# Hedgehog attention and Fourier mixing: the first fold on VectorE, rows first, and the mean subtraction on ScalarE

## The chip, the cores and the metric

The kernel runs on one core of one Trainium2 chip. The metric is the device time of one execution in microseconds. A core has five engines with a queue of instructions each: TensorE (PE in the profile; its weight loads are PEld), VectorE (DVE), ScalarE (ACT), GpSimd (POOL) and SyncE (SP). Here SyncE only issues transfers, and GpSimd issues transfers and computes. An engine works through its own queue in order; engines wait for one another through semaphores.

## The reference

There are 8 batches of 8 heads, 576 positions and head size 64. Attention without softmax comes first, then a Fourier mixing and a two-layer network:

```python
def phi(x):                                   # x is q or k
    proj = einsum('bhsd,df->bhsf', x, w_phi)  # 64 -> 128 features
    proj = proj - max(abs(proj), axis=-1, keepdims=True)
    return concatenate([exp(proj), exp(-proj)], axis=-1)
kv  = einsum('bhsf,bhsd->bhfd', phi(k), v)
z   = sum(phi(k), axis=2)
x   = einsum('bhsf,bhfd->bhsd', phi(q), kv) / (einsum('bhsf,bhf->bhs', phi(q), z)[..., None] + 1e-06)
# heads side by side: x is (8, 576, 512)
u   = x + real(fft(fft(x, axis=1), axis=2))
un  = (u - mean(u)) / sqrt(var(u) + 1e-06)    # over the last axis
out = u + maximum(un @ w_ch1, 0) @ w_ch2      # 512 -> 2048 -> 512
```

## The kernel before, in words

**Batches and streams.** A batch's work is cut into streams of small steps, each a Python generator. `PLAN`, a string with one letter per step, is the order in which all steps of all batches are recorded, and so the order of every engine's queue: nothing is reordered afterwards. Letters that matter here: `F` the two-layer network (`forward`, 68 steps), `M` the heads and the mixing (`mixing`, 26 steps), `D` the second fold (`fold_later`), `N` mean subtraction and transposes (`normalise`, one step per chunk of rows), `U` the scales (`scales`), `K`, `V`, `Q` the loads, `T` the exponentials of keys and queries, `R` and `P` the maxima, `S` the scaling of the values, `Y` matmuls on ones whose result nobody uses. While the network of one batch runs, the plan puts the attention and mixing of the next one between its steps.

**Rows.** A batch's 576 rows lie in five chunks of up to 128 partitions, in an order in which chunks 0 and 2, and 1 and 3, hold mirrored rows. X (128 x 5 x 513, f32) holds them all; its last column is a spare one.

**Attention.** `keys`, `queries` and `qmax` project on TensorE, ScalarE makes the exponentials KPp, KPn, QPHP, QPHN, VectorE takes maxima, GpSimd multiplies the values by the keys' scales into VCp, VCn, V4P, V4N (L460, L475). `keyvalue` sums kv (L896); a ScalarE copy makes it kvh. `combine` (L1018) multiplies a head's queries with it; VectorE adds and inverts (L1029, L1034, L1036), GpSimd writes the head's 64 columns of X (L1037).

**Mixing.** The real part of the two Fourier transforms is computed by matrix products with cosine and sine tables after folding: entries that share a cosine are added, those that share a sine subtracted, so that the products are half as large. From batch 1 on, GpSimd folds columns first (L1002): as soon as heads h and 7 - h stand in X, it writes their sums and differences to FEO (128 x 5 x 2 x 256, f32), two instructions of 320 elements each per pair of heads. VectorE then folds rows (`fold_rows`, L909 and L913) in two steps `D`. In batch 0 VectorE makes both. ScalarE copies one row to HI, TensorE spreads it over all partitions (pm, L1062), VectorE subtracts it (L1066), and a second fold along columns makes CEO (L1075). TensorE multiplies by the tables along rows (psD, L1086) and along columns (pu, L1141); VectorE adds the result to X (L1131), which now holds u.

**Normalise.** For each chunk, in the order 0, 2, 1, 3, 4, VectorE takes mean and variance (L1210, L1211) and, from batch 1 on, subtracts the mean into UN, in bf16 with columns reversed on both sides (L1186); SyncE issues a DMA that writes UN transposed to UT (L1203). Batch 0 subtracts with ScalarE (L1181, one chunk with VectorE) and transposes on TensorE. The scale 1/sqrt(var + 1e-06) is made by GpSimd with an addition (L1223) and a power (L1224), twice per batch: for chunks 0 and 2, and for all five.

**Network.** `hidden(0, 256)` multiplies UT of chunks 0 and 2 with W1b (psf, L1253) in 16 groups of four matmuls; ScalarE clips each group to HT (L1257). `output(0)`, `output(2)` follow, then `hidden(256, 576)` and the other three outputs (pso, L1264; the last chunk L1289). VectorE scales and adds to X (L1270, L1296), and SyncE stores the chunk: eight DMAs for chunk 1 (L1234), one or two for the others. psf, pso and pu share three PSUM buffers (`pb`), projections two others (`pj`).

**Loads.** GpSimd issues the loads of the next batches (L289): K in three pieces, V in six, Q in four.

Of the kernel before, what the change touches and what calls it, by code (L numbers as in the profile page):

```python
# [10 lines left out]
ALU = mybir.AluOpType  # L11
# [12 lines left out]
    "CYYYYYCZGZGTGRZZTZGGJKKTSTJRTPTRPYTQKSRJTYQPTJTRJMWTMPSSTPTPTMMTMTTPSCMMMTMVMMTMQTHYVMMMVMHHMHYYMYYZ"  # L24
    "MDDBMYAMHTMMVHRWMTMTNTMMTYYNNMNKSNFRFNFNFFUTFFFURSNTMTPFFNFUFMRTSPFTFRTNMSFFUFVTKQUMFFFMTFFSMFVKQTPT"
    "MFQUFFTBFPPMTPUAMTFFPMMFFMTFFMRFTFMFRFFFMFTFQFFMFPFMFFFFPFPFTFDFDQRKFFMVFTFMTFYFKVFTVMFFTMVKFRSSRMFT"
    "PPMTFTMNQNTFMSMSSBMMVTFTFMUTPMTMFNFMFNFMFFNFTUMFFFPTFFMKVFMMFFFMFFMFFFAMTRTVFFMRTSFFFFFFMFFFFTMVRFFF"
    "FTQPDFFFTPFFRDFFFTMKPQFFTMFKFFMMFFSRFMTFFVFMTTMTNNVFTFFFSFFMMMMTFMFBTPPQMSFFTFFTSPUNKMNFFVMFFMFFPNFF"
    "UMTFKFMFMFMFFFMFFFMFAMFFTRTFFMSFFFFQFRMFFTFFFTPRFFFFTMFFFTPDKFFFFDFFFRTMVTFFFMFMFQFFMVSRMFFFMTTTMTFF"
    "VNTMFSFNMVMMFTFFMTPSFFTBSFFVUMTPPFMFFFNNMTFPQFNFMFFUMFFKMFFPMFFKMFFMFFMFFAMFFFMTRTFFFMFFFRFFTMFFFTPF"  # L30
    "FFQRFDTFKPFFDFFFMQMFTFFMFFRMSFFTVTFMSRFFFMVTTTMTFNNMMVFMMFFSFTBMVNTTFTFSMFPFSUFFTFMTFFMNPPQPFMFKFFMF"
    "NFMUFKFPFMMFFAFFMFMFQFFTTMFFFRFSFMFFFFRFMFFFTFTPRFVFFFFMTFFDQKFPTRFFFDFFFVTMTFFFMFQMMSRFFTFFMFTTFVMT"
    "MFNFNFMMVSFTSMMTTFTFMFBTFTFFPFUMSFFMPPNPVNVAMFFFMFFMNFFMFFPMMFFFFFMFFMFTMRFFFTPSFFFFMFFFFVRMFFTFFTVP"
    "RFFFFMTDFFUFTPFFRFDFFFVTMTFFFMFMFFFMMFSRFTFMFMTNSTNTFSMMFFMMFTFFNMTTTFFFFNPPUMFFSTNMFFFMFFMTPFMFFUFP"
    "FFFMMFFFMFFMFFMFFMFMFFFMFFFFFFFMFFFFFFFDDFFFFMFFFMFMFFMMFFMFFMNNFFFFMUFFFMFFFFFFFMFFNFNFNFFFFFUFFFFF"
    "FFFFFFFFFFFFFFFFFFFFFFFFFFFFFFFFFFFFFFFFFFFFFFFFFFFFF"
# [4 lines left out]
def kernel(  # L41
# [41 lines left out]
    mhalf = const.tile([128, 5], F32, name="mhalf")  # L83
    nc.vector.memset(mhalf[:], -0.5)
# [41 lines left out]
    warm = const.tile([128, 1], F32, name="warm")  # L126
    keep = const.tile([128, 1], F32, name="keep")
# [163 lines left out]
    def make_k(b):  # L291
        KS = stage.tile([128, H, 256], BF16, tag="KS", name="KS")
        KS4 = stage.tile([64, H, D], BF16, tag="KS4", name="KS4")
        pieces = [(KS4[:], k[b, :, 512:576, :].rearrange("h p d -> p h d"))]
        for g in range(2):
            hs = slice(4 * g, 4 * g + 4)
            pieces.append(
                (KS[:, hs, :], k[b, hs, 0:512, :].rearrange("h (p j) d -> p h (j d)", j=4))
            )
        return (KS, KS4), pieces  # L300
# [606 lines left out]
    def fold_rows(FEO, lo, hi):  # L907
        odd = slice(max(lo, 1), hi)
        nc.vector.tensor_tensor(  # L909
            out=FEO[:, 2:4, 1, odd], in0=FEO[:, 0:2, 1, odd], in1=FEO[:, 2:4, 1, odd],  # L910
            op=ALU.subtract,
        )
        nc.vector.tensor_tensor(  # L913
            out=FEO[:, 2:4, 0, lo:hi], in0=FEO[:, 0:2, 0, lo:hi], in1=FEO[:, 2:4, 0, lo:hi],
            op=ALU.add,
        )
        if lo == 0:
            nc.gpsimd.tensor_tensor(
                out=FEO[:, 2:4, 1, 0], in0=FEO[:, 0:2, 1, 0], in1=FEO[:, 2:4, 1, 0], op=ALU.add
            )  # L920

    def first_heads():
        X = xpool.tile([128, 5, C + 1], F32, tag="X", name="X")
        FEO = fpool.tile([128, 5, 2, 256], F32, tag="FEO", name="FEO")
        CEO = fpool.tile([128, 3, 2, 2, 128], BF16, tag="CEO", name="CEO")
        HI = HIS[0]

        def rows_folded():
            nc.scalar.copy(out=HI[0:1, :, 1:128], in_=FEO[0:1, 0, :, 1:128])
            fold_rows(FEO, 1, 128)  # L930
            yield
# [479 lines left out]
```

## Time and profile before

| | us |
|---|---|
| median of 7 runs | 436.16 (433.82 to 439.5) |
| profiled execution | 436.59 |
| its span, first to last instruction | 434.8 |
| busy in it: TensorE | 406.7 |
| VectorE | 337.4 |
| ScalarE | 289.3 |
| GpSimd | 283.5 |
| mean granted TensorE clock | 0.979 |

Matmuls are pipelined, so a busy TensorE is not TensorE at its full pace. The idle time that a group shows is the engine's wait just before it, with what ended it. Instructions that only issue a transfer on SyncE are not counted as busy, but they take time on that queue. A clock of 0.50 in a stretch means that matmuls there ran at half speed.

### The profile page before, as it was taken

The numbers are of one execution on the slowest core, as the hardware profiler recorded it, in microseconds if no ns is written. First come the engines' busy times: TensorE is split into PE (matmuls) and PEld (weight loads), VectorE is DVE, ScalarE is ACT, GpSimd is POOL, SyncE is SP. The second block draws the span as 40 slices with busy tenths as digits, with TensorE's granted clock in tenths as the row PEclk, the third lists the DMA queues.
The fourth block names the chain that finished last, engine by engine and source line by source line (L and its number), as shares of the span: only waits on it lengthen the run. The fifth ranks groups of instructions, "written<-read, shape, count | busy, mean of one in ns | idle before, by whom it ended". The sixth has DMA issues, their size and how long they took to land.

```text
span 434.8 us, 10443 instructions
## 1 busy us (share of the span) xinstructions
PE 406.7 (94%) x4110; PEld 257.1 (59%) x4110; DVE 337.4 (78%) x643; ACT 289.3 (67%) x620; POOL 283.5 (65%) x386
## 2 busy tenths in 40 slices
PE   8699889999599999999999999999999989999993
PEld 3356466644285657665676558565766567656561
DVE  6978865799969988788979898887889796759102
ACT  2788799727664977577856897498757785344340
POOL 7886356898938976887579488797468453901100
PEclk9789999999889999999999999999999999999997
DMA  8999874939494398938692779938863171104304
GB/s 216 177 181 183 129 110 47 173 42 154 92 113 78 48 129 125 153 51 92 117 160 45 74 117 125 114 53 117 118 111 50 20 105 32 26 0 79 65 22 84
DMA packets 108962, 42.70 MB, mean 98 GB/s; under 512 B 83185, under 2 KB 103793, under 8 KB 108913
## 3 DMA queue, kind: packets, MB, share of 16 engines
q0 software_dynamic: 46272, 16.60, 35.4%
q1 hardware_dynamic: 62481, 25.38, 30.9%
q8 instruction: 32, 0.52, 0.5%
q14 instruction: 17, 0.14, 0.1%
q10 hardware_dynamic: 160, 0.07, 0.1%
HBM read 36.77 MB, written 9.44 MB: 106 GB/s over the span
## 4 chain that ended last, share of the span: by engine, by line
PE 55%; DVE 24%; ACT 9%; POOL 6%; DMA 3%; issue 1%; DVEq 0%; POOLq 0%; ACTq 0%
PE psf L1253 23%; PE pso L1264 17%; DVE X L1131 4%; DVE UN L1186 3%; DMA UT<-UN 3%; PE psD L1086 3%; POOL FEO L1002 2%; ACT HT L1257 2%; PE kv L896 2%; DVE st L1210 2%; POOL X L1037 1%; DVE CEO L1075 1%; ACT KPp L506 1%; PE psk L500 1%; DVE cb L1034 1%
## 5 line engine op out<-in xcount | busy, mean ns | idle before, releaser
L1253 PE MATMUL psf<-UT,W1b 128*128 128x320 bf16 (+1 forms) x1024 | 143.0, 288 | 8.4 <-DVE X L1296 4.2
L1257 ACT ACTIVATE HT<-psf 128x256 bf16<-128x256 f32 (+1 forms) x256 | 101.4, 417 | 53.9 <-PE psf L1253 45.9
L1264 PE MATMUL pso<-W2b,HT 128*128 128x512 bf16 x512 | 126.0, 379 | 0.0
L1253 PEld LDWEIGHTS <-W1b 128*128 128x128 bf16 x1024 | 95.2, 98 | 36.9 <-issue 8.0
L1264 PEld LDWEIGHTS <-HT 128*128 128x128 bf16 x512 | 45.7, 98 | 44.7 <-issue 2.5
L1037 POOL TENSOR_TENSOR X<-cb,rd 128x320 f32<-128x320 f32 x56 | 40.3, 726 | 22.8 <-DVE rd L1036 22.1
L475 POOL TENSOR_TENSOR VCn<-VS,VCn 128x512 bf16<-128x512 bf16 x28 | 29.7, 1060 | 30.7 <-ACT VCn L470 25.6
L1002 POOL TENSOR_TENSOR FEO<-X 128x320 f32<-128x320 f32 x56 | 46.3, 847 | 2.2
L1270 DVE SCALAR_TENSOR_TENSOR X<-pso,rs,X 128x512 f32<-128x512 f32 x32 | 23.6, 736 | 31.0 <-PE pso L1264 30.9
L506 ACT ACTIVATE KPn<-psk 128x1024 bf16<-128x1024 f32 x28 | 28.5, 1020 | 16.8 <-DVE MK L520 16.8
L564 DVE TENSOR_REDUCE MQ<-psq 128x8 f32<-128x1024 f32 (+1 forms) x32 | 34.3, 1087 | 4.9 <-PE psq L556 4.6
L506 ACT ACTIVATE KPp<-psk 128x1024 bf16<-128x1024 f32 x28 | 28.7, 1025 | 9.0 <-PE psk L500 8.9
L520 DVE TENSOR_REDUCE MK<-psk 128x8 f32<-128x1024 f32 x28 | 33.8, 1207 | 0.7 <-ACT KPp L506 0.6
L615 ACT ACTIVATE QPHP<-psh 128x1024 bf16<-128x1024 f32 x28 | 29.1, 1040 | 4.5 <-PE psh L606 4.4
L289 POOL DMA_DIRECT2D VS<-in_v_dram x42 | 30.1, 722 | 0.4 <-POOL VCp L475 0.3
L475 POOL TENSOR_TENSOR VCp<-VS,VCp 128x512 bf16<-128x512 bf16 x28 | 30.2, 1080 | 0.0
L615 ACT ACTIVATE QPHN<-psh 128x1024 bf16<-128x1024 f32 x28 | 29.4, 1048 | 0.0
L1210 DVE BATCH_NORM_STATS2 st<-X 128x6 f32<-128x512 f32 (+1 forms) x40 | 27.2, 680 | 0.0
L1223 POOL TENSOR_SCALAR VE<-MV 128x2 f32<-128x2 f32 (+1 forms) x16 | 5.7, 354 | 32.8 <-DVE MV L1211 31.9
L1186 DVE TENSOR_SCALAR UN<-X,MV 128x512 bf16<-128x512 f32 (+1 forms) x35 | 25.4, 727 | 1.3
L1131 DVE TENSOR_TENSOR X<-pu,X 128x512 f32<-128x512 f32 (+3 forms) x49 | 23.2, 527 | 3.6 <-PE pu L1141 3.4
L289 POOL DMA_DIRECT2D QS<-in_q_dram x28 | 23.8, 855 | 1.4 <-DMA QT<-QS 1.4
(460 smaller groups left out, 807.2 us busy)
## 6 DMA issues: line engine op xcount, KB each, us to landing
out_dram<-X SPq DMA_DIRECT2D x16, 256.0 KB
out_dram<-X SPq DMA_DIRECT2D x64, 64.0 KB
KS<-in_k_dram POOLq DMA_DIRECT2D x14, 256.0 KB, 5.0
QS<-in_q_dram POOLq DMA_DIRECT2D x14, 256.0 KB, 5.2
VS<-in_v_dram POOLq DMA_DIRECT2D x28, 128.0 KB, 3.8
W1b<-in_moe_w_ch_dram POOLq DMA_DIRECT2D x1, 2048.0 KB, 15.8
W2b<-in_moe_w_ch_dram POOLq DMA_DIRECT2D x1, 2048.0 KB, 15.4
W2b<-in_k_dram SPq DMA_DIRECT2D x2, 512.0 KB
```

Source lines behind the costliest of these rows:

```text
L289: nc.gpsimd.dma_start(out=pieces[i][0], in_=pieces[i][1])
L475: nc.gpsimd.tensor_tensor(out=VC[:, hs, :, 0:D], in0=values[b][0][:, hs, :].rearrange("p h (j d) -> p h j d", d=D), in1=VC[:, hs, :, D:D + ...
L506: nc.scalar.activation(out=KP[:, hs, :, :].rearrange("p e (jp jj) f -> p jj (e jp) f", jj=2), in_=psk[:], func=AT.Exp, scale=sgn,)
L615: nc.scalar.activation(out=o, in_=psh[:], func=AT.Exp, scale=sgn)
L1002: nc.gpsimd.tensor_tensor(out=FEO[:, :, i, a:a + D], in0=X[:, :, a:a + D], in1=X[:, :, C - a:C - a - D:-1], op=op,)
L1037: nc.gpsimd.tensor_tensor(out=X[:, :, D * h:D * h + D], in0=cb[:, :, 0:D], in1=rd[:].to_broadcast([128, 5, D]), op=ALU.mult,)
L1131: nc.vector.tensor_tensor(out=to, in0=more, in1=to, op=ALU.add)
L1186: nc.vector.tensor_scalar(out=UN[0:M, c, ::-1], in0=X[0:M, c, C - 1::-1], scalar1=mv[0:M, c, 0:1], scalar2=None, op0=ALU.subtract,)
L1210: nc.vector.bn_stats(out=st[0:M, :], in_=X[0:M, c, 0:C])
L1253: nc.tensor.matmul(ps[:], lhsT=W1b[:, cc, 128 * hh:128 * hh + 128], rhs=UT[:, cc, lo:hi], start=(cc == 0), stop=(cc == NCC - 1),)
L1257: nc.scalar.activation(out=HT[:, hh, lo:hi], in_=ps[:], func=AT.Relu)
L1264: nc.tensor.matmul(po[:], lhsT=HT[:, hh, at:at + 128], rhs=W2b[:, hh, :], start=(hh == 0), stop=(hh == NHH - 1),)
```

## The change

- **First fold.** From batch 1 on GpSimd's folds by pairs of heads go. For all batches `folded` runs on VectorE, rows first: four steps `D` instead of two. The first two add and subtract the mirrored chunks for the outer and the inner columns (four instructions of 512 elements), the third folds the single chunk 4 along columns and lets ScalarE copy the row to HI in two parts, the fourth folds the rest along columns. The result R is 128 x 3 x 2 x 512.
- **Subtraction.** From batch 1 on VectorE only negates the mean (nm), and ScalarE subtracts: one instruction per chunk.
- **Loads and scales.** K comes in two pieces, V in four; there is one power per batch from batch 1 on, and the addition before it is VectorE's.
- **Order.** `PLAN` is another string: 1236 steps instead of 1253, since some streams have fewer. Heads are combined in the order 0, 7, 1, 6, 4, 2, 5, 3 instead of 4, 0, 7, 1, 6, 2, 5, 3.

```diff
-    def fold_rows(FEO, lo, hi):
...
+    def folded(X, R, HI):
+        by_row = (ALU.add, ALU.subtract)
+        quarters = X[:, :, 0:C].rearrange("p c (a n) -> p c a n", n=128)
+        for cs in (slice(0, 4, 3), slice(1, 3)):
+            for i, op in enumerate(by_row):
+                nc.vector.tensor_tensor(
+                    out=R[:, 0:2, i, :].rearrange("p c (a n) -> p c a n", n=128)[:, :, cs],
+                    in0=quarters[:, 0:2, cs], in1=quarters[:, 2:4, cs], op=op,
+                )
+            yield
+        for i, op in enumerate(by_row):
+            nc.vector.tensor_tensor(
+                out=R[:, 2, i, 1:256], in0=X[:, 4, 1:256], in1=X[:, 4, 511:256:-1], op=op
+            )
+            nc.vector.tensor_tensor(
+                out=R[:, 2, 0, 256 * i:256 * i + 1], in0=X[:, 4, 0:1], in1=X[:, 4, 256:257], op=op
+            )
+        flat = HI[0:1].rearrange("p i n -> p (i n)")
+        nc.scalar.copy(out=flat[:, 0:257], in_=R[0:1, 2, 0, 0:257])
+        nc.scalar.copy(out=flat[:, 257:512], in_=R[0:1, 2, 1, 1:256])
+        yield
+        for i, op in enumerate(by_row):
+            nc.vector.tensor_tensor(
+                out=R[:, 0:2, i, 1:256], in0=R[:, 0:2, i, 1:256], in1=R[:, 0:2, i, 511:256:-1],
+                op=op,
+            )
...
-        def fold(h):
-            a = D * h
-            for i, op in enumerate((ALU.add, ALU.subtract)):
-                nc.gpsimd.tensor_tensor(
-                    out=FEO[:, :, i, a:a + D], in0=X[:, :, a:a + D],
-                    in1=X[:, :, C - a:C - a - D:-1], op=op,
-                )
...
-        nc.vector.scalar_tensor_tensor(
-            out=flat[0:65, 4, :], in0=flat[0:65, 4, :], scalar=keep[0:65], in1=pm[0:65],
-            op0=ALU.mult, op1=ALU.subtract,
-        )
+        for i, n in ((0, 257), (1, 255)):
+            nc.vector.scalar_tensor_tensor(
+                out=R[0:65, 2, i, i:i + n], in0=R[0:65, 2, i, i:i + n], scalar=keep[0:65],
+                in1=pm[0:65, 257 * i:257 * i + n], op0=ALU.mult, op1=ALU.subtract,
+            )
...
                 measure(b, c)
-                nc.vector.tensor_scalar(
-                    out=UN[0:M, c, ::-1], in0=X[0:M, c, C - 1::-1], scalar1=mv[0:M, c, 0:1],
-                    scalar2=None, op0=ALU.subtract,
+                nm = small.tile([128, 1], F32, tag="nm", name="nm")
+                nc.vector.tensor_scalar_mul(out=nm[0:M, :], in0=mv[0:M, c, 0:1], scalar1=-1.0)
+                nc.scalar.activation(
+                    out=UN[0:M, c, :], in_=X[0:M, c, 0:C], func=AT.Identity, bias=nm[0:M, :]
                 )
...
+            if b and first:
+                continue
...
-            nc.gpsimd.tensor_single_scalar(out=VE[:], in_=mv[:, cs, 1], scalar=1e-06, op=ALU.add)
+            nc.vector.tensor_single_scalar(out=VE[:], in_=mv[:, cs, 1], scalar=1e-06, op=ALU.add)
...
-        values[b], pieces = make_v(b, 4)
-        for which in ((0, 1), (2,), (3,), (4,), (5,)):
+        values[b], pieces = make_v(b, 2)
+        for which in ((0, 1), (2,), (3,)):
...
-        "F": (forward, 68), "M": (mixing, 26), "D": (fold_later, 2), "N": (normalise, 5),
-        "U": (scales, 2), "P": (part(0), 7), "T": (part(1), 18), "R": (part(2), 5),
-        "S": (part(3), 5), "K": (fetch_k, 3), "V": (fetch_v, 5), "Q": (fetch_q, 3),
+        "F": (forward, 68), "M": (mixing, 26), "D": (fold_later, 4), "N": (normalise, 5),
+        "U": (scales, 1), "P": (part(0), 7), "T": (part(1), 18), "R": (part(2), 5),
+        "S": (part(3), 5), "K": (fetch_k, 2), "V": (fetch_v, 3), "Q": (fetch_q, 3),
```

## The prediction

> **What bounds the kernel now.** I read the page's busy shares and clock row first, then TensorE's waits, then the timeline around the longest wait, then SyncE's timeline, and the groups by shape last.
>
> ```profile
> PE 406.7 (94%) x4110; PEld 257.1 (59%) x4110; DVE 337.4 (78%) x643; ACT 289.3 (67%) x620; POOL 283.5 (65%) x386
> PEclk9789999999889999999999999999999999999997
> ```
>
> TensorE is busy nearly always; VectorE is second. The clock row dips in three places: slices 2 and 3, slices 11 and 12, the end.
>
> The chain of waits ends in TensorE alone. It gives TensorE's pace when nothing holds it:
>
> ```profile
> 397.33 6.29 PE psf L1253 x56
> 403.62 6.91 PE pso L1264 x32
> 410.53 8.69 PE psf L1253 x64
> ```
>
> So 112 ns for 256 columns, 136 for 320, 216 for 512. Both kernels issue the same matmuls (the same counts of every shape in their built orders), so the time changes only by how long TensorE is held. Its waits, longest first (us in total, times, longest):
>
> ```profile
> PE psf L1253 <- DVE X L1296: 4.2, 1, 4.2
> PE psf L1253 <- DMA UT<-UN: 2.8, 5, 0.9
> ...
> PE psD L1086 <- DVE CEO L1075: 1.9, 3, 1.1
> ```
>
> The single large one is in batch 1. VectorE and TensorE there (start, duration; the bracket is the idle time before):
>
> ```profile
> 112.57 4.65 DVE L1186 TENSOR_SCALAR UN<-X,MV 128x512 bf16<-128x512 f32 x1
> 117.14 1.93 DVE L1131 TENSOR_TENSOR X<-pu,X 128x512 f32<-128x512 f32 x4
> 119.00 1.52 DVE L1296 SCALAR_TENSOR_TENSOR X<-pso,rs,X 64x512 f32<-64x512 f32 x2
> ```
> ```profile
> 119.80 1.44 PE L1253 MATMUL psf<-UT,W1b 128*128 128x256 bf16 x6 [4.24 <-DVE X L1296]
> ```
> ```profile
> 112.74:116.15 3.41, 1.98 (x40) 1.32 (x38) 3.41 (x1) 3.38 (x8) 3.41 (x5) 1.00 0.27 44
> 116.15:122.98 6.83, 3.18 (x23) 2.43 (x24) 6.69 (x11) 1.03 (x3) 4.23 (x6) 0.50 0.79 60
> ```
>
> One mean subtraction took 4.65 us while GpSimd ran six products on end. The last two lines (stretch, then busy PE, PEld, DVE, ACT, POOL, granted clock) show GpSimd busy throughout, and the clock at 0.50 from 116.15 to 122.98. The subtraction's usual price (min/median/max ns), and that of two-input folds by shape (busy us, mean ns | idle before):
>
> ```profile
> L1186 DVE TENSOR_SCALAR UN<-X,MV x35: 478/486/4649, 110.8 to 401.5; 128x512 bf16<-128x512 f32 x28, 64x512 bf16<-64x512 f32 x7
> ```
> ```profile
> L1075 DVE TENSOR_TENSOR CEO<-FEO 128x384 bf16<-128x384 f32 x24 | 13.0, 568 | 0.2
> L913 DVE TENSOR_TENSOR FEO<-FEO 128x384 f32<-128x384 f32 x7 | 6.4, 920 | 0.0
> ```
>
> From batch 2 on, the transposes of the first chunks stand on SyncE's queue behind eight stores of one chunk:
>
> ```profile
> 158.45 5.93 SPq L1234 DMA_DIRECT2D out_dram<-X  x8
> 164.49 2.59 SPq L1203 DMA_TRANSPOSE UT<-UN  x2
> ```
>
> The second UN had ended at 162.57 (162.06 + 0.51), 1.9 us before its queue was free.
>
> **The change part by part.** The sum is made against the profiled execution's own 436.59 us (span 434.8 and 1.8 around it); it stands 0.43 above the median of 436.16.
>
> *Mean subtraction to ScalarE, batch 1.* In the changed order VectorE runs, from the first addition after the second projection to the second chunk's mean: additions 0.68 + 0.15 + 0.68, statistics 0.68 + 0.18, the new negation 0.15 (nm rows of batch 0: 135 to 152 ns), a 64-row maximum 1.21, statistics 0.86, negation 0.15: 4.74. Then UN on ScalarE, 0.72 (batch 0's row, 707 to 743 ns), behind half an exponential of 1.04, then 2.58 to the first psf (119.80 less 117.22). From 108.60, where those additions start, that is 117.16 instead of 119.80: **-2.6**; -3.2 with nothing in front, -2.1 behind a whole exponential. What is late next is this same transpose, TensorE waiting about 1.6.
>
> *The clock.* 3.18 us of matmuls after 119.80 ran at 0.50: 1.6 lost. The ends are 0 (the drop came after a stretch in which TensorE was busy only 1.98 of 3.41, partly because ScalarE was full) and -1.6. I take **-1.6**: the stall that filled the slow stretch mostly goes, and the changed order puts the last block of four filler matmuls (0.86) between these projections.
>
> *Mean subtraction, batches 2 to 7.* VectorE loses 28 times 789 less 486 ns, 8.5 us in all, to blocked subtractions; 4.2 of it is the one above. The rest gives TensorE nothing: the first two chunks wait for SyncE, whose stores are in the same place in the changed queue. Behind these transposes on SyncE stand K's and the last stores, which a late UN would hold too. If the cover goes, two UNs on ScalarE behind an exponential cost at most 1.8 per batch. TensorE's work between the end of the output that those stores follow and the first psf, at the paces above, is 9.1, 8.8, 8.9, 8.6, 8.4 us for batches 2 to 6 before and 9.8, 8.3, 8.8, 9.3, 8.1 after: even. **0**; ends -2.8 (the whole transpose wait) and 6 times 1.8 = +10.8.
>
> *ScalarE's new work.* Five UNs of 0.72 per batch, seven batches: 25 us on 289. Two chunks lie in the projections; three fall mostly into the next batch's first hidden layer, where each psf group (four matmuls, 0.44) waits for a ScalarE eviction (0.39) and has three buffers. Two spare buffers cover 0.88: one UN alone, but not UN plus exponential (1.76), 0.88 short. Ends: 0, and three such meetings in each of six batches, 15.8. By the windows ScalarE idles a quarter of the time (178.8 busy of 250 from 125 to 375), so I take one meeting in twelve: **+1.3**.
>
> *Folds.* Off GpSimd go 56 folds (46.3 us), 7 corner sums (3.0) and 7 column copies (1.3). On VectorE, per batch: four of 512 elements, between the unblocked rows of 384 (0.55) and 640 (0.82), 0.68 each; two of 255 at 0.41 (batch 0's rows of 254 and 256); two of 510 at 0.68; four tiny at 0.15 (the two-column additions); the subtraction of pm in two of about 0.45 for one of 0.74. That is 5.5 plus 0.2. It loses the old row folds, 0.74 + 0.92 + 0.28 + 0.28 = 2.2, and UN, 25.4/7 = 3.6, and gains five negations and one epsilon, 0.9: +0.8 per batch on an engine idle 16% (209.6 of 250, so 7.5 us in a period of some 47). The path from the last head's product to pm was 1.69 (two GpSimd folds) + 0.56 + 0.61 (HI) = 2.9; it becomes 1.36 + 1.12 + 0.8 (two HI copies at the 0.41 of a one-row copy) = 3.3, and the new last fold step, 1.7, runs beside HI and pm and adds about 0.8 ahead of the CEO folds. TensorE's order leaves 9.9, 9.1, 9.9, 6.0, 8.0, 6.0 us there (7.2, 5.9, 7.7, 5.4, 5.3, 6.0 before), 1.9 more on average than it had. **0**; ends -1.9 (the CEO wait goes) and +4: if GpSimd blocks four folds on the path, each by 0.53 (what separates blocked and free L913, 1.08 and 0.55), 2.1 per batch against 1.9 of new cover leaves 0.2, or 0.6 where only 1.5 is new, in seven batches.
>
> Here a rule speaks against the change. The row: L913 averages 920 ns where L1075 of the same 384 elements averages 568. The Trainium skill (SBUF — State Buffer, "SBUF: two separate sides") says VectorE instructions with two SBUF inputs and GpSimd share one port pair as an exclusive lock, held for a whole instruction, and that the loser waits it out. By the rule alone every fold on the path may lose a whole product of 0.73: four make 2.9 per batch against 1.9 of new cover, +7, and 440.3. By the rows only some pairs meet a product, and it stays at 433.3.
>
> *Fewer loads, one root.* Three DMA issues (0.72 to 0.80 each) and one root (0.74) less per batch on GpSimd, and the epsilon: 3.3 us. GpSimd sets no TensorE wait in the list; **0**. SyncE's transposes of K now wait for one larger load, whose issue stands early enough; at worst the 5.0 us landing of 256 KB doubles, still before its use a batch later. The single root's scales are due only at the first output, eight steps of the forward pass later.
>
> *Start, batch 0.* The 512-element mask on VectorE took 3.04 (10.55 to 13.59) while GpSimd cleared six buffers; a 960-element one took 0.66. The changed GpSimd order issues a load after three of them: -1.3 (0 to -2.3). Against it: the last fold runs 4.0 instead of 3.06 before pm's subtraction (+0.9), and ScalarE copies HI ahead of three of the four sine tables, so that their 2.3 us and the next table load stand between HI and the next evictions (+0.4; 0 to +1.8). **0**; ends -2.3 and +2.7.
>
> Sum: -2.6 - 1.6 + 1.3 = -2.9; 433.7 beside the own 436.59, **433.3** beside the median.
>
> **Rivals.** *ScalarE becomes what holds the hidden layers* (slower). For it: only 0.05 us of spare per group. Against: ScalarE's idle quarter. At one and a half short meetings per batch (1.3 us) it costs 7.9 in six batches, less 4.2: **439.8**. It decides from 0.7 per batch on, where it eats the gain. *The stall re-forms*: ScalarE's exponentials, full in 112.74 to 116.15 (3.38 of 3.41), make the second UN as late as the lock did, the clock drops again, and SyncE hides the rest: **436.2**. *The port lock falls on the folds*: the +4 above in place of 0: **437.3**, or nearer 434 if half of them meet a product.
>
> **How the numbers follow.** A measurement tells about 0.5% from no change, 2.2 us. Forecast 0.45 (0.38 faster, 0.07 same); ScalarE 0.27 (0.25 slower); re-formed stall 0.18 (0.12 same, 0.04 slower); lock 0.10, spread evenly. Faster 0.42, same 0.25, slower 0.33. The forecast's own range, from its ends for stall and start, is 430 to 435.5; with the cases of both signs it is 428.5 to 441.
>
> **What would show it.** Right: no TensorE wait over 2.5 us in batch 1, no clock of 0.50 between batch 0's start and the end, UN at 0.72 on ScalarE, GpSimd near 205 us busy, folds of 512 near 0.68. Wrong: waits of psf for HT or for UN above 1 us in several batches; folds of 512 near 1.2; the start later than now at the first psf.

## The result and the profile after

The changed kernel takes 438.25 us (median of 14 runs, 436.66 to 439.15), the kernel before 436.23 us in 35 runs beside it: a ratio of 1.0041, with a 95% interval of 1.0024 to 1.0057. That is slower by 0.4%, inside the 2.2 us (0.5%) within which the prediction counts a time as the same. It had forecast 433.3, faster, with 430 to 435.5 as the range of the forecast. The profiled execution took 437.48 us, its span is 435.7.

The page of the changed kernel: the busy shares, the clock row, and the group of the moved mean subtraction (busy us, mean ns | idle time of ScalarE just before it, and what ended it).

```profile
PE 406.1 (93%) x4110; PEld 254.7 (58%) x4110; DVE 339.8 (78%) x720; ACT 308.4 (71%) x661; POOL 208.6 (48%) x269
PEclk9999999999999999999999999999999999999998
L1152 ACT ACTIVATE UN<-X,nm 128x512 bf16<-128x512 f32 (+1 forms) x35 | 25.0, 723 | 10.7 <-DVE nm L1151 9.9
```

Nearly everything that was to show the forecast right is there: UN costs 0.72 us on ScalarE, GpSimd is busy 208.6 us (near 205 was said), and the clock row has no dip between its ends. TensorE's waits (us in total, times, longest) no longer hold the 4.2 us of batch 1:

```profile
PE psf L1220 <- DMA UT<-UN: 3.8, 4, 1.6
PE psD L1050 <- DVE CEO L1039: 1.9, 4, 0.7
...
PE psk L496 <- DVE cb L1004: 0.9, 2, 0.5
...
PE psh L602 <- ACT KPn L502: 0.7, 1, 0.7
...
PE pm L1026 <- ACT HT L1224: 0.7, 1, 0.7
...
PE psk L496 <- ACT KPn L502: 0.4, 1, 0.4
```

No single wait stands out; there are more short ones. The timeline around batch 1's projections, where one subtraction had taken 4.65 us on VectorE and TensorE had stood 4.24 us, now reads (start, duration; the bracket is the idle time before):

```profile
109.21 0.72 ACT L1152 ACTIVATE UN<-X,nm 128x512 bf16<-128x512 f32 x1
111.14 1.08 POOL L471 TENSOR_TENSOR VCp<-VS,VCp 128x512 bf16<-128x512 bf16 x1
111.28 0.72 ACT L1152 ACTIVATE UN<-X,nm 128x512 bf16<-128x512 f32 x1 [0.44 <-DVE nm L1151]
114.76 1.47 PE L1220 MATMUL psf<-UT,W1b 128*128 128x256 bf16 x10
```

The second subtraction ran beside a GpSimd product (111.14) in its usual 0.72, and the first psf followed without a long wait. TensorE's pace at the end of the chain is the old one (64 psf in 8.69 us), and on SyncE the eight stores still stand ahead of the first transposes, here in batch 3:

```profile
411.47 8.69 PE psf L1220 x64
```
```profile
200.07 5.13 SPq L1201 DMA_DIRECT2D out_dram<-X  x8
205.30 3.62 SPq L1168 DMA_TRANSPOSE UT<-UN  x2
```

The second subtraction ended at 205.19 on ScalarE (204.47 + 0.72), just as the queue came free (200.07 + 5.13 is 205.20): in this batch the cover that the prediction counted on held, with nothing to spare. So the stall is gone, and yet the kernel is not faster. The milestones tell why. The table gives the start of each batch's first psf by the two timelines, in us:

| batch | 0 | 1 | 2 | 3 | 4 | 5 | 6 | 7 | span |
|---|---|---|---|---|---|---|---|---|---|
| before | 55.1 | 119.8 | 168.4 | 213.9 | 261.5 | 308.4 | 355.2 | 395.6 | 434.8 |
| after | 52.2 | 114.8 | 162.8 | 210.3 | 260.9 | 306.4 | 354.9 | 396.7 | 435.7 |

The changed kernel leads by 2.9 us at batch 0's first psf, by 5.0 at batch 1's and 5.6 at batch 2's, and has lost it all by batch 7. The matmuls ahead of batch 1's first psf are the same work in both orders (about 80.1 and 79.8 us at the paces of 112, 136 and 216 ns for 256, 320 and 512 columns and estimated ones for the small products), so that point cuts both kernels into comparable halves: **119.8 and 315.0 us before, 114.8 and 320.9 after; 5.0 gained, 5.9 lost.** The cut puts the 3.2 us at half clock behind the old stall (119.8 to 122.98) into the second half of the kernel before. The prediction priced them at 1.6, and the changed kernel has no such drop, so what else it lost there is nearer 7.5 than 5.9. In the second half I took each matmul's end, less the end of the one before it and its own pace, and put what was left down to the engine that had released it: what ScalarE ended rose from 3.0 to 6.8 us, what the transposes on SyncE ended from 3.8 to 4.5, and what VectorE ended by 0.9 to 1.6, depending on the pace taken for the small products.

### The profile page after: what moved, and what is told of

Read it like the earlier page. It is cut to its first block, busy times and chain, and to the rows that moved or that the text cites. A ratio compares the mean times of both kernels' runs of the same rounds, so it can differ in the third digit from the quotient of the medians.

```text
span 435.7 us, 10470 instructions
## 1 busy us (share of the span) xinstructions
PE 406.1 (93%) x4110; PEld 254.7 (58%) x4110; DVE 339.8 (78%) x720; ACT 308.4 (71%) x661; POOL 208.6 (48%) x269
## 4 chain that ended last, share of the span: by engine, by line
PE 48%; DVE 31%; ACT 13%; DMA 3%; POOL 3%; issue 2%; DVEq 0%; POOLq 0%; ACTq 0%; SPq 0%
PE psf L1220 22%; PE pso L1231 12%; DVE cb L1004 4%; DVE tg L999 3%; DMA UT<-UN 3%; DVE MK L516 2%; DVE R L908 2%; DVE X L1095 2%; PE kv L892 2%; PE psD L1050 2%; ACT HT L1224 2%; DVE X L1237 2%; DVE st L1175 2%; ACT KPn L502 2%; ACT QPHN L611 1%
## 5 line engine op out<-in xcount | busy, mean ns | idle before, releaser
L1224 ACT ACTIVATE HT<-psf 128x256 bf16<-128x256 f32 (+1 forms) x256 | 100.0, 416 | 34.2 <-PE psf L1220 26.9
L502 ACT ACTIVATE KPn<-psk 128x1024 bf16<-128x1024 f32 x28 | 28.6, 1022 | 13.8 <-DVE MK L516 13.7
L1152 ACT ACTIVATE UN<-X,nm 128x512 bf16<-128x512 f32 (+1 forms) x35 | 25.0, 723 | 10.7 <-DVE nm L1151 9.9
L456 POOL TENSOR_TENSOR V4N<-VS,V4N 64x256 bf16<-64x256 bf16 x14 | 8.9, 638 | 48.1 <-ACT V4N L452 34.5
L1191 POOL TENSOR_TENSOR rs<-VE,mhalf 128x5 f32<-128x5 f32 (+1 forms) x9 | 10.3, 1139 | 33.5 <-DVE VE L1190 33.5
L992 PEld LDWEIGHTS <-QPHP 128*128 128x128 bf16 x280 | 20.8, 99 | 5.6 <-DVE cb L1004 2.1
```

The costliest lines, as they stand in the source:

```text
L502: nc.scalar.activation(out=KP[:, hs, :, :].rearrange("p e (jp jj) f -> p jj (e jp) f", jj=2), in_=psk[:], func=AT.Exp, scale=sgn,)
L1224: nc.scalar.activation(out=HT[:, hh, lo:hi], in_=ps[:], func=AT.Relu)
```

## The experiments

The theory that came out of this: moving the subtraction to ScalarE made ScalarE's other evictions late (A, G in the texts below). Rivals: waiting at the head of ScalarE's queue (F), VectorE's new folds (C, H), and the changed order of steps itself (B, I, J, K). All kernels were timed beside the kernel before; for most, the two halves of its profiled span are given too, cut at batch 1's first psf. The halves are of one execution, the time is the median of several: the profiled one took 3.8 us more than the median in the first run below, 2.9 more with the folds alone in the old order, 1.9 more with only the folds on GpSimd, 4.8 more in "before, then changed" and 2.0 less with the subtraction back on VectorE.

### The subtraction, in both orders

*All of it on ScalarE, in the order of before.*

```diff
-                nc.vector.tensor_scalar(
-                    out=UN[0:M, c, ::-1], in0=X[0:M, c, C - 1::-1], scalar1=mv[0:M, c, 0:1],
-                    scalar2=None, op0=ALU.subtract,
-                )
+                nm = small.tile([128, 1], F32, tag="nm", name="nm")
+                nc.vector.tensor_scalar_mul(out=nm[0:M, :], in0=mv[0:M, c, 0:1], scalar1=-1.0)
+                nc.scalar.activation(
+                    out=UN[0:M, c, :], in_=X[0:M, c, 0:C], func=AT.Identity, bias=nm[0:M, :]
+                )
```

> The kernel before with one thing done: the mean subtraction of batches 1 to 7 as a negation on VectorE and an activation on ScalarE; its order of steps, folds, loads and roots kept. The prediction's terms for this part alone were -2.6 (batch 1's stall), -1.6 (clock) and +1.3 (ScalarE): 433.3. Theory A: the stall and the clock go, but ScalarE costs 3.8 and not 1.3: 435.8 (434.5 to 437). Rival B (order is what costs): the gain stands whole, 432. Both expect no TensorE wait over 2.5 us in batch 1; if the stall is still there, the lock was not its cause.

Measured: 452.97 us, ratio 1.0386 (1.0357 to 1.0416); halves 117.5 and 337.4. Neither theory had it. In the profiled execution the first half gains 2.3 us and the second loses 22, of which 3.8 is that execution's distance from the median. The timeline of this run in batch 2 shows the mechanism:

```profile
169.55 0.15 DVE L1187 TENSOR_SCALAR nm<-MV 128x1 f32<-128x1 f32 x1
...
169.74 0.72 ACT L1188 ACTIVATE UN<-X,nm 128x512 bf16<-128x512 f32 x1 [2.56 <-DVE nm L1187]
...
170.37 0.25 ACT L904 CAST kvh<-kv 128x130 bf16<-128x130 f32 x1
...
170.67 0.40 PE L896 MATMUL kv<-VCp,KPp 128*128 128x65 bf16 x4 [2.64 <-ACT kvh L904]
```

ScalarE had nothing to do for 2.56 us. The subtraction stood first in its queue and waited for the negated mean, which VectorE reached late (a maximum of 1.23 and the statistics came first); the copy of kvh, 0.25 us of work that was ready, stood behind it; and TensorE stood 2.64 us for kvh. Over the run this wait is the largest:

```profile
PE kv L896 <- ACT kvh L904: 13.7, 12, 3.8
```

The clock adds to it: it stood at 0.51 from 169.6, within the wait shown, to 176.5, and again from 323.2 to 330.1; from batch 2 on the kernel before has no such drop until its end.

*The same, over 64 of 512 columns.*

```diff
-                    out=UN[0:M, c, :], in_=X[0:M, c, 0:C], func=AT.Identity, bias=nm[0:M, :]
+                    out=UN[0:M, c, 0:64], in_=X[0:M, c, 0:64], func=AT.Identity, bias=nm[0:M, :]
```

> The kernel before with the mean subtraction on ScalarE in all seven batches, but over 64 of 512 columns only (seven eighths of the subtraction are left out): ScalarE's work for it falls from 25 us to about 9, while each one still waits for VectorE's negated mean, with what stands behind it in ScalarE's queue. The full one gave 453.0, 16.4 us over the kernel before, and ScalarE stood idle 16.5 us ahead of subtractions. Theory F (the queue's head waiting is the cost): 446 to 451. Rival G (ScalarE's added work is the cost): 437 to 441.

Measured: 447.10 us, ratio 1.0244 (1.0220 to 1.0268); halves 117.2 and 327.6. The short activation took 0.35 us, so ScalarE lost some 12 us of work (it is busy 296.1 us instead of 308.6), and 5.9 of the 16.4 us went. 10.7 us over the kernel before stayed: most of the price is waiting at the head of the queue, as theory F said, and a third is the work. The group's idle time in this run shows that the waiting did not shrink with the work, it grew (16.5 us in 18 waits before the cut):

```profile
  DVE nm L1189: 21.1, 24
```

*ScalarE's subtraction cut in the changed order.* The same edit, made in the changed kernel.

> The changed kernel with the subtraction over 64 of 512 columns only (seven eighths left out): ScalarE loses some 16 us of its 308, its queue's waits for the negated mean (9.9 us) stay. Theory G (added work on ScalarE makes its evictions late): 434.5 (433 to 436). Theory F (waiting at the queue's head), or that the order is what costs: 437 to 438.3.

Measured: 437.95 us, ratio 1.0036 (1.0020 to 1.0051); halves 115.0 and 321.0, the second that of the changed kernel to a tenth. ScalarE is busy 298.4 us instead of 308.4. Theory A/G falls: in the changed order these 10 us of ScalarE's added work cost TensorE nothing that can be measured. ScalarE's waits for the negated mean stayed (9.3 us here, 9.9 in the changed kernel), so this run does not price them.

*The subtraction back on VectorE, in the changed order* (the first diff of this section, reversed).

> The changed kernel with one thing undone: the mean subtraction of batches 1 to 7 back on VectorE, in the changed order. In the changed kernel's trace the waits of TensorE that end with a ScalarE instruction came to 6.8 us from batch 1's first psf on, against 3.0 before (+3.8); those that end with VectorE to 4.4 against 2.8 (+1.6). Theory A (the subtraction on ScalarE makes evictions late): the +3.8 goes, the time falls to 434.5 (433 to 436), with ScalarE-ended waits near 3. Rival B (the new order of steps is what costs, whichever engine subtracts): 438, no change from the changed kernel. Rival C (VectorE is what holds TensorE, so that 35 more instructions of 0.49 to 0.79 there cost more than they save on ScalarE): 440 or more, VectorE-ended waits over 6.

Measured: 449.30 us, ratio 1.0281 (1.0256 to 1.0305); halves 116.1 and 329.4. It is 11 us slower than the changed kernel, so A falls here too, but not to C as it was put: what VectorE ended has one large entry.

```profile
160.13 4.86 DVE L1150 TENSOR_SCALAR UN<-X,MV 128x512 bf16<-128x512 f32 x1
160.62 1.06 POOL L471 TENSOR_TENSOR VCn<-VS,VCn 128x512 bf16<-128x512 bf16 x1
161.63 1.05 POOL L471 TENSOR_TENSOR VCp<-VS,VCp 128x512 bf16<-128x512 bf16 x1
162.65 1.05 POOL L471 TENSOR_TENSOR VCn<-VS,VCn 128x512 bf16<-128x512 bf16 x1
163.66 1.05 POOL L471 TENSOR_TENSOR VCp<-VS,VCp 128x512 bf16<-128x512 bf16 x1
...
165.71 0.62 PE L1255 MATMUL pso<-W2b,HT 128*64 128x512 bf16 x2 [5.03 <-DVE X L1095]
```

The stall of batch 1 has come back, in batch 2: again one subtraction sits on VectorE until GpSimd's run of products ends (164.7), and TensorE stands 5.03 us. The clock stood at 0.50 for 3.4 us behind it (165.8 to 169.2). These two make most of the 8.5 us by which this run's second half is the longer one.

*Only batch 1's first two subtractions on ScalarE, in the order of before.*

```diff
+                if b == 1 and c in (0, 2):
+                    nm = small.tile([128, 1], F32, tag="nm", name="nm")
+                    nc.vector.tensor_scalar_mul(out=nm[0:M, :], in0=mv[0:M, c, 0:1], scalar1=-1.0)
+                    nc.scalar.activation(
+                        out=UN[0:M, c, :], in_=X[0:M, c, 0:C], func=AT.Identity, bias=nm[0:M, :]
+                    )
+                else:
+                    nc.vector.tensor_scalar(
...
```

> The kernel before with the mean subtraction on ScalarE for batch 1's first two chunks alone. With all 35 on ScalarE in this order the stretch from batch 0's last output to batch 1's first hidden-layer product was 1.8 us shorter (13.1 to 11.3). If the stall and the clock were worth what the prediction said: -2.6 - 1.6, so 432. If only what that stretch showed, and the clock's drop goes too: about 434. Rival: ScalarE's two subtractions put the projections' and batch 1's features behind them, and the time is 436 or more.

Measured: 434.21 us, ratio 0.9935 (0.9911 to 0.9959); halves 117.6 and 314.8. The stall itself is worth 2.2 us. The clock's drop did not go (columns: stretch, then busy PE, PEld, DVE, ACT, POOL, granted clock, DMA share, GB/s):

```profile
111.67:115.08 3.41, 1.41 (x16) 0.69 (x17) 3.07 (x6) 3.41 (x8) 3.36 (x4) 1.00 0.67 95
115.08:121.91 6.83, 6.09 (x61) 4.76 (x61) 5.01 (x10) 4.29 (x11) 5.73 (x9) 0.51 0.78 137
```

TensorE is still busy only 1.41 of 3.41 us there, now because ScalarE is full (3.41 of 3.41) and its exponentials are late, and the next 6.83 us run at 0.51. The clock dropped behind TensorE's idle time in that stretch, though something else had caused it.

### The two orders

*The changed operations in the old order, and the folds alone in it.* Both use the old PLAN with each letter D written twice. The first has the changed operations, with empty steps where they need fewer; two powers per batch are kept:

```diff
-        "U": (scales, 1), "P": (part(0), 7), "T": (part(1), 18), "R": (part(2), 5),
-        "S": (part(3), 5), "K": (fetch_k, 2), "V": (fetch_v, 3), "Q": (fetch_q, 3),
+        "U": (scales, 2), "P": (part(0), 7), "T": (part(1), 18), "R": (part(2), 5),
+        "S": (part(3), 5), "K": (fetch_k, 3), "V": (fetch_v, 5), "Q": (fetch_q, 3),
...
-    LONGER = {("N", 0): 10, ("U", 0): 7, ("M", 0): 24, ("T", 0): 20}
+    LONGER = {("N", 0): 10, ("U", 0): 7, ("M", 0): 29, ("T", 0): 20}
```

The second is the kernel before with the changed `folded` and the heads that call it:

```diff
-        "F": (forward, 68), "M": (mixing, 26), "D": (fold_later, 2), "N": (normalise, 5),
+        "F": (forward, 68), "M": (mixing, 26), "D": (fold_later, 4), "N": (normalise, 5),
```

> The changed kernel's operations in the order of steps of the kernel before (the two steps of the row folds doubled to four, empty steps where there are fewer, two roots per batch kept since one would come too late in batch 5). Theory A: the subtraction on ScalarE and the folds cost the same or more without an order made for them: 438 to 442. Rival B: the old order is the better one, so 433 or less.

> The kernel before with the folds alone moved to VectorE, in its order (the two steps of the row folds doubled to four at their place; subtraction, loads and roots as before). All of the change in this order was 28.8 us over the subtraction alone (481.8 against 453.0), with TensorE waiting 12.1 us at pm for evictions ahead of the copy of HI. Theory J (parts priced by the order they stand in): 450 to 462, the waits at pm there without any subtraction on ScalarE. Rival (the two parts only hurt together): under 442.

Measured: all of the change 481.81 us, ratio 1.1017 (1.0991 to 1.1043), halves 123.0 and 357.0; the folds alone 461.19 us, ratio 1.0569 (1.0542 to 1.0597), halves 127.3 and 335.0. The second is what theory J expected; for the first, neither theory came near. So in the order of before the folds cost 25 us, the subtraction 16, and all together 45. With the folds alone, the waits are at pm, as theory J said:

```profile
PE pm L1036 <- ACT HT L1231: 12.0, 5, 2.9
PE pm L1036 <- ACT HI L926: 4.9, 2, 2.8
```

The clock is part of the 25 us: its mean over this run is 0.957, against 0.979 before. In that order pm comes too early for a fold chain on VectorE. By the trace the time from the last head's product on GpSimd to the end of the second HI copy was 5.2 to 7.5 us in batches 1 to 6, since up to three maxima of 1.2 stand between the folds on VectorE, and TensorE stood 1.7 to 2.9 in each. In the changed kernel the same chain took 3.1, 7.3, 6.8, 7.7, 3.4, 4.4 and 3.3 us in batches 1 to 7, and TensorE stood at most 0.65 for pm. This is the cover that the prediction worked out (5.3 to 7.7 us of TensorE work ahead of pm before, 6.0 to 9.9 after), and the changed order does supply it. The chain's price of 3.3 us was too low: with it, the old order would have covered the folds as well.

*The operations of before in the changed order, and the folds alone put back in it.* The changed PLAN; the folds of before, in four steps of which two are empty, and, from the second of these kernels on, the changed order of heads:

```diff
-        order = (4, 0, 7, 1, 6, 2, 5, 3)
-        ready = {7: (0,), 6: (1,), 5: (2,), 3: (3,)}
+        order = (0, 7, 1, 6, 4, 2, 5, 3)
+        ready = {6: (1,), 4: (0,), 5: (2,), 3: (3,)}
```

> The kernel before with all its operations (folds on GpSimd, subtraction on VectorE, more loads, two roots) in the changed order of steps; steps that are now fewer are joined, and where there are more a step is empty. Rival B: the order costs some 4 us by itself, 440. Theory A: nothing of the +3.8 is there; 435 (433 to 438), the GpSimd folds falling in other places are the open part. A stall of one subtraction behind GpSimd products may turn up in another place.

> All operations of the kernel before in the changed order, with the heads taken in the changed order (in the first attempt head 4 came ahead of its features and took those of the batch before). Theory J: 450 to 460, most of it in stalls behind GpSimd; if the order alone were the loss: 440.

> The changed kernel with the folds alone put back on GpSimd (with VectorE's row folds, as before), in the changed order and its order of heads. Theory H (VectorE's fold work costs some 5 us here): 433 if GpSimd had room; but the steps are placed for folds of VectorE, so the fold of the last head now comes after two more GpSimd products in the queue ahead of pm: theory J (a part is priced by the order it stands in) says 445 to 455, with TensorE or VectorE waiting for GpSimd's FEO.

Measured: 458.71 us with the old order of heads (1.0496, 1.0474 to 1.0519), where head 4 comes ahead of its own features, and 458.22 (1.0503, 1.0489 to 1.0516) with the changed order of heads; 440.49 us with only the folds on GpSimd (1.0106, 1.0089 to 1.0123; halves 115.6 and 324.9). The first two say that neither order is the better one by itself: the old operations lose 22 us in the new order (the first of these runs had been expected at 440 at most), and the new ones 45 in the old. The third is a surprise in its smallness: it was expected at 445 to 455, and is 2.2 us over the changed kernel. VectorE is the better place for the folds in this order, but by little.

### What the lost half is made of

*The folds cut to an eighth.*

```diff
-    def folded(X, R, HI):
+    def folded(X, R, HI, n=128):
...
-                    in0=quarters[:, 0:2, cs], in1=quarters[:, 2:4, cs], op=op,
+                    in0=quarters[:, 0:2, cs, 0:n], in1=quarters[:, 2:4, cs, 0:n], op=op,
...
-                out=R[:, 0:2, i, 1:256], in0=R[:, 0:2, i, 1:256], in1=R[:, 0:2, i, 511:256:-1],
+                out=R[:, 0:2, i, 1:2 * n], in0=R[:, 0:2, i, 1:2 * n], in1=R[:, 0:2, i, 511:512 - 2 * n:-1],
...
-        folds[b] = folded(X, R, HI)
+        folds[b] = folded(X, R, HI, 16)
```

> The changed kernel with VectorE's folds of batches 1 to 7 cut: those of 512 elements to 64, those of 510 to 62 (seven eighths of them are left out), the instructions and their order the same. VectorE loses about 3 us per batch, 20 in all. With the subtraction cut in the same way nothing moved (437.95 against 438.25). Theory H (VectorE's fold work makes the maxima and the CEO folds late, and through them the exponentials and TensorE): the 5.7 us lost after batch 1's first hidden layer mostly come back, 433 to 435. Rival I (the loss is in where the changed order puts steps, whatever they cost): 437 to 438.3.

Measured: 432.99 us, ratio 0.9921 (0.9900 to 0.9941); halves 113.2 and 318.0. VectorE is busy 318.7 us instead of 339.8, and the kernel is 5.3 us faster than the changed one. Of this, 1.5 lie in the first half and 3.0 in the second (the rest is between the changed kernel's profiled run and its median). The first half would show more: this run had a drop of the clock at its start that the changed kernel's profile lacks, and from batch 0's first psf to batch 1's it took 60.1 us against 62.6. One chain shows the way that it takes. The changed kernel while batch 3's outputs and batch 4's mixing run:

```profile
245.32 1.91 DVE L1039 TENSOR_TENSOR CEO<-R 128x381 bf16<-128x381 f32 x2
...
247.65 1.21 DVE L516 TENSOR_REDUCE MK<-psk 128x8 f32<-128x1024 f32 x1
...
248.90 1.02 ACT L502 ACTIVATE KPn<-psk 128x1024 bf16<-128x1024 f32 x1 [1.82 <-DVE MK L516]
...
249.97 0.39 PE L602 MATMUL psh<-QT,wphi 64*128 64x512 bf16 x2 [0.74 <-ACT KPn L502]
```

and the same instructions with the folds cut:

```profile
242.43 1.47 DVE L1040 TENSOR_TENSOR CEO<-R 128x381 bf16<-128x381 f32 x2
...
244.32 1.21 DVE L516 TENSOR_REDUCE MK<-psk 128x8 f32<-128x1024 f32 x1
...
245.57 1.02 ACT L502 ACTIVATE KPn<-psk 128x1024 bf16<-128x1024 f32 x1 [0.54 <-DVE MK L516]
...
246.64 0.39 PE L602 MATMUL psh<-QT,wphi 64*128 64x512 bf16 x2
```

In the changed kernel VectorE goes without a break from the folds to CEO to the next head's maximum; ScalarE idles 1.82 us for that maximum; its exponential is late; and TensorE waits 0.74 us before the next features. The trace names ScalarE as the releaser, and so did my first theory, but the late engine is VectorE, one step behind. With short folds ScalarE idles 0.54 there and TensorE does not wait. The waits for CEO shrink with it, from 1.9 us in four to one:

```profile
PE psD L1051 <- DVE CEO L1040: 0.7, 1, 0.7
```

The folds themselves were hardly held by GpSimd; in the changed kernel they took (busy us, mean ns | idle before)

```profile
L908 DVE TENSOR_TENSOR R<-X 128x512 f32<-128x512 f32 x32 | 22.0, 738 | 0.1
...
L1039 DVE TENSOR_TENSOR CEO<-R 128x384 bf16<-128x384 f32 x24 | 13.7, 597 | 0.2
...
L925 DVE TENSOR_TENSOR R<-R 128x510 f32<-128x510 f32 x16 | 10.2, 680 | 0.0
```

with a median of 0.683 for the first: 1.8 us in all over 32 of them.

*Both cuts*, this one and that of the subtraction to 64 columns, in the changed kernel.

> The changed kernel with both cuts: the subtraction over 64 of 512 columns on ScalarE, and VectorE's folds of batches 1 to 7 over an eighth (seven eighths of both left out). Folds alone gave 433.0, the subtraction alone 437.95. Theory K (the rest of the loss is in the order's placement): 432.5 to 433.5, no more than the folds alone. Rival G (ScalarE's added work costs once VectorE isn't in the way): 429 to 431.

Measured: 434.28 us, ratio 0.9941 (0.9923 to 0.9958); halves 113.2 and 319.3. That is 0.8 above the range of theory K. The 1.3 us by which the second half is longer than with the folds cut alone go with the clock: in this profile it stood at 0.50 from 209.3 to 212.7, in the other one it did not. The one execution that was granted 0.998 took 431.93 us; the two with the folds cut alone and the same clock took 431.44 and 431.95. So the subtraction cut as well gains nothing, and ScalarE's work does not cost more once VectorE has room. That is theory K as far as it goes: cutting the folds gives back 3 of the 5.9 us lost, cutting the subtraction's work none, and the other 3 came back with neither cut. What the folds on GpSimd cost in the order of before was not measured, so the 3 us are the price of fold work on VectorE in this order, not of the move. By stretches the other 3 lie ahead of batch 3's first psf (TensorE stands 2.5 us beyond its matmuls from batch 2's last output on, 1.3 before) and in the first hidden layers of batches 3 and 5 (1.7 and 2.2, against 0.8 and 0.9). These values were 2.5, 1.7 and 2.2 with short folds as well, and 1.7 and 2.2 in the hidden layers with the short subtraction. The two transposes in batch 3, 3.62 us against 3.07 before, are 0.55 of it. Theory K puts the rest down to where the changed order places steps. That is not shown: fewer and larger loads, the single power, and ScalarE's waits for the negated mean are in all these kernels, and no run takes one of them away by itself. Of the last, the trace of the changed kernel shows little: only one TensorE wait of 0.15 us or more in the second half (0.76, for a transpose, at 260.87) ends within 2.5 us after such a wait.

*The two halves put together the other ways.* The steps of one order up to a point, then the steps of the other that are not yet done; the operations of a batch follow the order that starts them (its folds the order in which its heads are combined).

```diff
+    def mixing(b):
+        yield from (mixing_n if b in NEW_M else mixing_o)(b)
...
+                if (b, c) in NEW_N:
+                    nm = small.tile([128, 1], F32, tag="nm", name="nm")
...
-        for i in range(2):
+        for i in range(2 if b in NEW_K else 3):
             load(pieces, (i,))
```

> The changed order and operations up to batch 1's first hidden-layer product, and from there the order and operations of the kernel before (steps already done are left out of it). Up to that product the changed kernel's TensorE stood still 4.7 us less than the one before (39.7 us beyond the matmuls' own time before, 35.0 after), and from there on 5.7 more (22.0 against 27.6). Theory D (the two halves are separate: a gain at the start and at batch 1's stall, a loss spread over batches 1 to 7 that comes with the changed order): 436.2 - 4.7 = 431.5 (430 to 433.5). Rival E (the loss is the other side of the gain, work put off or squeezed together, that must be made up later in any order): 435 to 437, no gain.

> The other half: the order and operations of the kernel before up to batch 1's first hidden-layer product, from there the changed ones. Theory D (separate halves): the old start and stall and the new loss, 436.2 + 5.7 = 442 (440.5 to 443). Rival E (gain and loss belong together): 437 to 438.5.

> The changed order and operations up to batch 2's first hidden-layer product, then the kernel before. By the waits up to there (45.1 us before, 40.1 after) 436.2 - 5.0 = 431.2; the cut at batch 1 gave 433.0, of which 1.2 were lost at the seam by the wait for the subtraction there. Theory D: 431 to 433. If the loss begins already in batch 1's hidden layers: 433.5 or more.

> The changed order and operations up to batch 2's mean product, then the kernel before. TensorE's waits up to there were 37.3 us in the changed kernel and 42.8 before: 436.2 - 5.5 = 430.7 by those; the cut at batch 2's first hidden-layer product was 431.2 by the same reckoning and came to 432.75, so 432 to 432.5 here, level with it.

Measured:

| kernel | us | ratio to before (95%) | halves |
|---|---|---|---|
| changed, then before (batch 1's first psf) | 433.00 | 0.9926 (0.9898 to 0.9954) | 117.8, 315.0 |
| changed, then before (batch 2's first psf) | 432.75 | 0.9923 (0.9903 to 0.9944) | 116.4, 314.6 |
| changed, then before (batch 2's pm) | 434.46 | 0.9958 (0.9944 to 0.9972) | 116.2, 316.0 |
| before, then changed | 442.99 | 1.0173 (1.0136 to 1.0209) | 124.1, 321.9 |

Gain and loss are separate (theory D): the changed start keeps most of its gain ahead of the old rest, whose length is the old one to 0.4 us in the first two, and the changed rest behind the old start is 1.0 us off its own length. (The 124.1 of that start is this execution's: the clock stood at 0.50 from 26.4 to 36.6 in it.) Rival E, that the loss is the other side of the gain, falls. Each splice has a price at its seam: 3.4 of the 4.7 us that the expectation reckoned with were kept at the first (436.37 beside it, less 433.00), and the third, by the same reckoning the best, was the worst of the three. The second beats both kernels, by 0.8% and 1.3%.

## Why the prediction was wrong, by its steps

*Mean subtraction to ScalarE, batch 1 (-2.6).* Right in mechanism and size: the two runs without the stall, in the old order, gained 2.2 (434.21) and 2.3 us (first half 117.5), and in the changed kernel the way from batch 0's first psf to batch 1's is 2.1 us shorter (62.6 against 64.7). "What is late next is this same transpose" did not hold in the changed order, where psf followed without it.

*The clock (-1.6).* Gone in the changed kernel, as forecast, but not for the reason given first. In the old order, with the stall gone, it dropped all the same, behind a full ScalarE. That is the second rival's full ScalarE and its drop of the clock, though the second subtraction itself was not late there (111.52 to 112.24). In the changed kernel TensorE was busy 6.19 of the 8.0 us from 107 to 115, and the clock stayed at 1.00; which of the moved steps did that was not tested.

*Start (0).* Wrong by 2.9 us at batch 0's first psf in the two profiles compared, outside the end given for it (-2.3). The mask on VectorE fell from 3.04 to 1.64 us, which was foreseen as -1.3. What was not: in this profile the clock's first drop went too (the windows' columns as above; the kernel before first, then the changed one), after TensorE's wait of 2.14 us for the copy queued behind that mask had gone.

```profile
17.20:24.00 6.80, 6.22 (x43) 2.86 (x42) 5.38 (x7) 5.58 (x9) 5.42 (x8) 0.50 0.98 127
```
```profile
17.20:24.00 6.80, 5.61 (x67) 3.06 (x66) 6.80 (x10) 6.67 (x14) 6.74 (x8) 1.00 1.17 113
```

The prediction had seen that dip in the clock row and priced only the other one. Part of the 2.9 is luck of the execution: of eight profiles that begin in the changed order with its operations, three have no drop there and reach batch 0's first psf at 52.2 to 52.5, and five have one of 3.4 us and reach it at 53.1 to 53.5, which is 1.6 to 2.0 gained and inside the end.

*Mean subtraction, batches 2 to 7 (0), and ScalarE's new work (+1.3).* ScalarE's work is near 0 in the changed order: cut to half its time, the subtraction gave back 0.3 us, less than the runs' spread. The ends were honest: in the old order the same instructions cost 16 us net. But the mechanism named for that end, too few spare psf buffers, was the small part of it: there psf waited 2.5 us for evictions, and kv 13.7. The price was a ready copy of kvh behind a subtraction that waited for VectorE, and the prediction asked what the moved instruction adds to ScalarE, not what it waits for there. *ScalarE becomes what holds the hidden layers* is refuted for the changed order, where no wait of psf for HT is in the list.

*Folds (0).* **This is the step that failed.** It priced the chain from the last head to pm, found it covered by the 1.9 us more of TensorE work that the changed order leaves there, and the cover held (pm waits twice for HI, 0.9 in all, and once 0.7 for an eviction), but with luck: the chain of 3.3 took up to 7.7 us, for it had no maxima in it. It counted 0.8 us per batch more for VectorE "on an engine idle 16%" and let that be free. The second halves (stretch, then busy PE, PEld, DVE, ACT, POOL, granted clock, DMA share, GB/s; before, after, and with the folds cut) show that VectorE's sum hardly rose, from 236.81 to 239.55 us:

```profile
119.80:426.10 306.30, 301.62 (x3006) 196.20 (x3008) 236.81 (x442) 203.42 (x446) 191.56 (x251) 0.99 0.60 83
```
```profile
114.80:427.10 312.30, 304.99 (x3020) 194.60 (x3018) 239.55 (x504) 222.15 (x489) 130.69 (x159) 1.00 0.56 82
```
```profile
113.20:422.70 309.50, 304.39 (x3020) 195.10 (x3018) 222.66 (x504) 221.67 (x489) 129.77 (x159) 1.00 0.56 82
```

What has a price is where the fold work stands. Measured, 21 us less of it are worth 5.3 us, 3.0 of them in the second half: the idle share is an average, and after the heads VectorE is full for some ten microseconds on end (from 238.2 to 248.9 in the stretch shown), with the maxima that ScalarE and TensorE need queued behind the folds. *The port lock falls on the folds* was the wrong reason for a loss of the right kind: the folds ran at 0.738 on average, and what they cost came mostly from their plain time. Folds on GpSimd are no way out in this order: they made it 2.2 us slower.

*What was left out.* The prediction took the order as neutral where it saw the same matmuls and even covers. Some 3 us of the second half are left for it and for the parts of the change that no run took alone; how they divide stays open.

The sum had gains of 4.2 (the stall and the clock) against a loss of 1.3. Measured, the stall and the start gave 5.0 up to batch 1's first psf, and behind it 5.9 went, the clock's gain already counted in.

## What to carry to other kernels

Where a hand-made order feeds in-order queues, an operation has no price of its own: here the same move of the subtraction cost 16 us in one order and saved 11 in the other. When you move an instruction to another engine, ask first what it will wait for at the head of the new queue and what stands ready behind it, and read an engine's idle share in the stretch where the work goes, not over the span. When a large change moves the time little, cut both traces at points where the same work is done: here a gain and a loss of 5 to 6 us each lay apart, and keeping the one without the other gave the fastest kernel.

## What the runs showed of the hardware

- The granted clock dropped behind an idle TensorE for two different causes of the idle time: with the blocked subtraction gone, a stretch of 3.41 us with TensorE busy 1.41 was followed by 6.83 us at 0.51. TensorE's longest wait in that stretch was 1.4 us. The Trainium skill (TensorE: Matmul & The Clock Gate, "Why this matters for your kernels") advises against idle gaps of more than about 3 us; here several short ones in one stretch had the same effect. It varies between executions: at the start, five of the eight profiles that begin in the changed order with its operations had 3.4 us at 0.50 and three had none.
- A subtraction on VectorE beside a run of GpSimd products waited out several of them, not one: 4.65 us in batch 1 before, where it ended 0.28 after the fifth of six (116.94), and 4.86 in batch 2 with the subtraction put back, where it ended 0.28 after the last (164.71). Folds with two inputs on VectorE met products as well and were longer by only 0.06 on average (0.738 against a median of 0.683).
- Cutting an activation on ScalarE from 512 to 64 columns took it from 0.72 to 0.35 us, and a fold on VectorE from 512 to 64 elements from 0.74 to 0.26: an eighth of the elements is half or a third of the time.
